# Head sums of a windowed attention by SBUF to SBUF DMA and VectorE adds instead of matmuls, and the softmax in the FFN2 stage

## The chip, the core and the metric

The kernel runs on one core of a Trainium2 chip. Its engines are TensorE (PE in the profile; its weight loads PEld), VectorE (DVE), ScalarE (ACT), GpSimd (POOL) and SyncE (SP, which here only issues DMAs). Each engine works through its own instructions in order, and waits on semaphores for the others. The metric is the device time of one execution in microseconds; the kernel before takes 1237.61 us, the median of three runs (1237.54 to 1237.85).

## What is computed

Two layers, each a windowed self-attention and a feed-forward network, both with a residual and a LayerNorm without scale or shift ahead of them. Sequence S = 2048, width D = 1024, 32 heads of 32, F = 3584, all inputs and the output bf16.

```
def attention(x):                                  # x: layernormed, [S, D]
    q, k, v = split(x @ wqkv)                      # [32 heads, S, 32]
    # token s sees the 8 tokens s, s-2, ..., s-14 (where >= 0)
    logits[h,s,w] = dot(q[h,s], k[h,s-2w]) / sqrt(32)     # else -1e9
    o[h,s] = sum_w softmax_w(logits)[h,s,w] * v[h,s-2w]
    return o.reshape(S, D) @ wo
def ffn(x):
    return gelu_tanh(x @ w1 + b1) @ w2 + b2
for _ in range(2):
    x = x + attention(layernorm(x));  x = x + ffn(layernorm(x))
```

## The kernel before

**Groups and stages.** The 2048 tokens are cut into four groups of T = 512; with two layers there are N = 8 group passes, n = 0 to 7, n mod 4 being the token group. One pass has four stages, each a generator that yields after every unit of TensorE work: gen_qkv (24 units of 8 matmuls: eight chunks of q, of k, of v), gen_wo (8 units of 8 matmuls), gen_ffn1 (28 units of 8), gen_ffn2 (32 units of 7). The stages are interleaved by the loop at the end of the kernel: wo(n), qkv(n+2), ffn1(n), ffn2(n). So the attention of group n+2 is prepared while the FFN of group n runs.

**Attention on VectorE.** The columns of wqkv are taken with a stride of 8, so chunk c of q, k and v holds the channels c, c+8, ... of all heads, and partition p belongs to head p // 4: HP = 4 partitions a head. new_prod(n, c) (L287) multiplies q of a chunk with the eight windows of k, [128 partitions, 8 windows, 512 tokens], into a "big" buffer, and adds the products of the eight chunks up in a tree: 8 multiplications and 7 additions of 4096 elements a partition. What remains is a sum over the four partitions of a head. That is head_sum (L272): eight matmuls with the 0/1 matrix smat, which put token block tb (128 tokens) on the PSUM partitions tb*32 to tb*32+31, one per head, giving L [128, 8, 128]. attend (L349) calls it, and then does the softmax over the windows: maximum, subtraction, exponential (ScalarE), sum, reciprocal and product, into a. spread (L368) copies a through DRAM into abc, so that each of the four partitions of a head has its weights (DMAs issued by POOL). av(n, c) (L381) multiplies abc with the windows of v and adds the eight windows up, into oT.

**Buffers.** "big" has 3 buffers (product tree, av). q, k, abc and oT have one each, v two. The accumulators in PSUM ("acc") are 6, taken in turn by all stages; L has its own. Weights "wt" have 5 buffers of 1 MB.

**Evictions.** gen_ffn2 takes four accumulators for the first half of the columns and four for the second (pss, L443). A half is finished only in its last four units, and VectorE then adds bias and residual: tmp<-acc, x<-tmp.

```
for dh in range(2):
    pss = [[acc_tile() for _ in p] for p in parts]
    for kq in range(4):
        for tt in range(NTT):   # 7 matmuls, one unit
```

**What sets the order.** TensorE's order is the program's: every matmul depends on the one before (L111). On VectorE, ScalarE, POOL and SP a scheduler places instructions, unless the wrapper InOrder (L82) binds them: hold() makes all later instructions of the engine come after the last one so far, and on = True keeps program order (always on for POOL, here). The side work of a stage is hung on units: at(u, f, ...) calls f after unit u, each(f, n, u0, du) calls f(n, c) after unit u0 + du*c. The lines that matter are these (ln_a is the LayerNorm that feeds a qkv, ln_stats_ahead its statistics):

```
stage(gen_ffn1(0), sides=at(4, attend, 1) + at(4, spread, 1) + at(4, hold) + each(new_prod, 2, 2, 1, 0, 4) + each(av, 1, 6, 2))
stage(gen_ffn2(0), sides=at(0, ln_stats_ahead, 3) + at(15, hold) + each(new_prod, 2, 15, 1, 4, 8) + at(23, hold) + at(23, ln_a, 3, None, True))
```

All engine calls go through one-line helpers, so in the profile nearly every instruction has line L93 (InOrder) or L118 (mm); it is told apart by the tiles it writes and reads.

Of the kernel before, what the change touches and what calls it, by code (L numbers as in the profile page):

```python
# [9 lines left out]
ALU = mybir.AluOpType  # L10
AX = mybir.AxisListType
BF16 = mybir.dt.bfloat16
F32 = mybir.dt.float32
# [4 lines left out]
def kernel(  # L18
# [18 lines left out]
    P = 128  # L37
    _, S, D = A_x.shape
    F = B_w1.shape[1]
    H = 32  # L40
    DH = D // H
    W = 8
    DIL = 2
    HALO = (W - 1) * DIL
# [3 lines left out]
    T = 512  # L48
    NTT = T // P
# [4 lines left out]
    HP = P // H  # L54
    N = NLAYER * NG
# [17 lines left out]
    bigp = ctx.enter_context(tc.tile_pool(name="bigp", bufs=3))  # L73
    dram = ctx.enter_context(tc.tile_pool(name="dram", bufs=2, space=bass.MemoryType.DRAM))
    smp = ctx.enter_context(tc.tile_pool(name="smp", bufs=1))
# [51 lines left out]
    def load_qkv(which):  # L127
        tiles = []
        for h in range(2):
            wt = wpool.tile([P, KD // 2, D], BF16, name="wt")  # L130
            sp.dma_start(wt[:], wqkv_v[:, h * (KD // 2):(h + 1) * (KD // 2), which * D:(which + 1) * D])
            tiles.append(wt)
        return tiles
# [121 lines left out]
    def win(t_ap):  # L255
        a = t_ap.ap
        assert len(a) == 2 and a[1][0] == 1 and a[1][1] == HALO + T
        return bass.AP(tensor=t_ap.tensor, offset=t_ap.offset, ap=[list(a[0]), [DIL, W], [1, T]])

    st = {n: {} for n in range(N)}  # L260
    xa = {}
    xb = {}
# [9 lines left out]
    def head_sum(n, last=True):  # L272

        if "L" not in st[n]:
            st[n]["L"] = psum.tile([P, W, P], F32, name="L", bufs=1)
            start = True
        else:
            start = False
        L = st[n]["L"]
        prod = st[n]["prods"].pop(0)  # L280
        for wh in range(2):
            for tb in range(NTT):
                mm(L[tb * H:(tb + 1) * H, wh * 4:(wh + 1) * 4, :], lhsT=smat[:],
                   rhs=prod[:, wh * 4:(wh + 1) * 4, tb * P:(tb + 1) * P], start=start,
                   stop=last, skip_group_check=True, tile_position=(0, tb * H))

    def new_prod(n, c):  # L287

        s = st[n]
        prod = bigp.tile([P, W, T], BF16, name="big")  # L290
        vec.tensor_tensor(out=prod[:], in0=s["qT"][:, c, :].unsqueeze(1).to_broadcast([P, W, T]), in1=win(s["kT"][:, c, :]), op=ALU.mult)
        tree = s["prods"]
        tree.append(prod)
        if c % 2 == 1:
            for _ in range(1 if c % (NCH // s["parts"]) == 1 else 2):
                b = tree.pop()
                vec.tensor_tensor(out=tree[-1][:], in0=tree[-1][:], in1=b[:], op=ALU.add)

    def gen_qkv(n, parts=1, defer=False, qk_pool=None, v_late=False, qk_next=None):
        g = n % NG  # L300
        xnT = xa.pop(n)
        s = st[n]
        s["parts"] = parts
        s["prods"] = []
        qk_pool = qk_pool or attp
        wq = wq_first if n == 0 else load_qkv(0)
        wk = load_qkv(1)
        if n == 0:
            ln_early(1)
            wv = load_qkv(2)  # L310
            ln_early(2, qk_next)
            load_x(3)
        qT = qk_pool.tile([P, NCH, T], BF16, name="qT")
        first = {}
        for kq in range(4 if n == 0 else 0):
            for c in range(6):
                first[c] = qkv_chunk(wq, c, xnT, first.get(c), kq * (KD // 4), (kq + 1) * (KD // 4), 0, 2)
                if (kq, c) in ((1, 5), (2, 5)):
                    transpose_on_pe(*first_late.pop(0))
        for c in range(NCH):  # L320
            ps = qkv_chunk(wq, c, xnT, first[c], t0=2) if c in first else qkv_chunk(wq, c, xnT)
            act.copy(qT[:, c, :], ps[:])
            yield
        if n > 0 and not v_late:
            wv = load_qkv(2)
        kT = qk_pool.tile([P, NCH, HALO + T], BF16, name="kT")
        s["qT"], s["kT"] = qT, kT
        act.copy(kT[:, :, 0:HALO], (zhalo if g == 0 else khalo)[:])
        for c in range(NCH):
            ps = qkv_chunk(wk, c, xnT)  # L330
            act.copy(kT[:, c, HALO:], ps[:])
            if not defer:
                new_prod(n, c)
            yield
        if g + 1 < NG:
            act.copy(khalo[:], kT[:, :, T:T + HALO])
        vT = attp.tile([P, NCH, HALO + T], BF16, name="vT", bufs=2)
        s["vT"] = vT
        if v_late:
            wv = load_qkv(2)  # L340
        act.copy(vT[:, :, 0:HALO], (zhalo if g == 0 else vhalo)[:])
        for c in range(NCH):
            ps = qkv_chunk(wv, c, xnT)
            act.copy(vT[:, c, HALO:], ps[:])
            yield
        if g + 1 < NG:
            act.copy(vhalo[:], vT[:, :, T:T + HALO])

    def attend(n):  # L349

        s = st[n]
        head_sum(n)
        L = s.pop("L")
        if n % NG == 0:
            vec.tensor_tensor(out=L[0:H, 0:W - 1, 0:HALO], in0=L[0:H, 0:W - 1, 0:HALO], in1=mask[:], op=ALU.add)
        mx = smp.tile([P, P], F32, name="mx")
        vec.tensor_reduce(out=mx[:], in_=L[:].rearrange("p w t -> p t w"), axis=AX.X, op=ALU.max)
        e = smp.tile([P, W, P], F32, name="e")
        vec.tensor_tensor(out=e[:], in0=L[:], in1=mx[:].unsqueeze(1).to_broadcast([P, W, P]), op=ALU.subtract)
        act.activation(e[:], e[:], ACT.Exp, scale=SCALE)  # L360
        z = smp.tile([P, P], F32, name="z")
        vec.tensor_reduce(out=z[:], in_=e[:].rearrange("p w t -> p t w"), axis=AX.X, op=ALU.add)
        vec.reciprocal(z[:], z[:])
        a = smp.tile([P, W, P], BF16, name="a")
        vec.tensor_tensor(out=a[:], in0=e[:], in1=z[:].unsqueeze(1).to_broadcast([P, W, P]), op=ALU.mult)
        s["a"] = a
# [45 lines left out]
    def gen_ffn1(n):  # L412
        xnT = xb.pop(n)
        hT = hpool.tile([P, KF, T], BF16, name="hT")
        st[("h", n)] = hT
        for j4 in range(KF // 4):
            wt = wpool.tile([P, KD, 4 * P], BF16, name="wt")
            load = sp.dma_start(wt[:], w1_v[:, :, j4 * 4 * P:(j4 + 1) * 4 * P])
            if n == 0 and j4 == 1:
                dep_order(load, last_transpose[0], "transposes first")  # L420
            for jj in range(4):
                j = j4 * 4 + jj
                ps = acc_tile()
                for k in range(KD):
                    mm(ps[:], lhsT=wt[:, k, jj * P:(jj + 1) * P], rhs=xnT[:, :, k, :], start=(k == 0), stop=(k == KD - 1))
                act.activation(hT[:, j, :], ps[:], ACT.Gelu_apprx_tanh, bias=b1T[:, j:j + 1])
                yield
# [63 lines left out]
    def stage(gen, count=None, sides=()):  # L491


        u = 0
        while count is None or u < count:
            if next(gen, gen) is gen:
                break
            for v, f in sides:
                if v == u:
                    f()  # L500
            u += 1
        for v, f in sides:
            if v >= u:
                f()

    def at(u, f, *args, **kwargs):
        return [(u, lambda: f(*args, **kwargs))]

    def each(f, n, u0, du, c0=0, c1=NCH):
        return [(int(u0 + du * (c - c0)), lambda c=c: f(n, c)) for c in range(c0, c1)]  # L510

    hold = vec.hold
# [5 lines left out]
    with tc.tile_pool(name="early", bufs=1) as early:  # L518
# [10 lines left out]
        hold()  # L529
        stage(q2, sides=each(new_prod, 1, 0, 1, 5, 8))  # L530
    hpool = ctx.enter_context(tc.tile_pool(name="hpool", bufs=1))
    stage(gen_ffn1(0), sides=at(4, attend, 1) + at(4, spread, 1) + at(4, hold) + each(new_prod, 2, 2, 1, 0, 4) + each(av, 1, 6, 2))
    stage(gen_ffn2(0), sides=at(0, ln_stats_ahead, 3) + at(15, hold) + each(new_prod, 2, 15, 1, 4, 8) + at(23, hold) + at(23, ln_a, 3, None, True))
    for n in range(1, N - 2):
        stage(gen_wo(n), sides=at(0, spread, n + 1) if n > 1 else at(7, attend, 2))
        stage(gen_qkv(n + 2), sides=(at(0, spread, 2) if n == 1 else []) + each(av, n + 1, 0, 2, 0, 3))
        stage(gen_ffn1(n), sides=at(20 if n == 1 else 9, attend, n + 2) + each(av, n + 1, 8, 2, 3, 8))
        if n + 3 < N:
            stage(gen_ffn2(n), sides=at(2, ln_a, n + 3))
        else:  # L540
            stage(gen_ffn2(n), sides=at(0, spread, n + 2) + each(av, n + 2, 1, 4))
    n = N - 2
# [35 lines left out]
```

## Time and profile before

| | |
|---|---|
| median of 3 runs | 1237.61 us (1237.54 to 1237.85) |
| profiled execution, its own time | 1237.71 us |
| its span, first to last instruction | 1236.0 us |
| TensorE busy | 1227.6 us, 99% |
| VectorE busy | 840.5 us, 68% |
| ScalarE busy | 303.8 us, 25% |
| GpSimd busy | 92.3 us, 7% |
| head-sum matmuls (64) | 4.9 us |
| HBM read | 197.40 MB |

How to read the lines of the profile: a group is a line, an engine, an operation and what it writes <- what it reads, with partitions x elements and type; then how often, busy time and mean of one, and the idle time of the engine just before, with what ended it. A timeline line begins with start and length in us; consecutive instructions of one kind are merged, and matmul records can be missing by a few per cent. The chain is the work that ended last, followed back from the end. Busy time of TensorE is modelled and doesn't say that it is at its peak.

### The profile page before, as it was taken

Reading aid. Unit: us, or ns where it says so; the run is one execution under the profiler, and the core shown is the slowest. Engines: PE = TensorE matmul, PEld = TensorE weight load, DVE = VectorE, ACT = ScalarE, POOL = GpSimd, SP = SyncE. Lnnn points to the kernel's source line nnn. Section 1 sums busy time; section 2 is a strip of 40 time slices with the busy share of each in tenths; the row PEclk is TensorE's granted clock in tenths of the full one; section 3 lists DMA queues with packets and bytes.
Section 4 is the critical chain, followed back from the end, with each engine's and each line's share of the span. In section 5 each row is a group of like instructions: output and inputs, shape, how many; then the busy total and the mean of one; then the engine's idle time right before and its main releaser. Section 6 shows DMA issues by size and latency. Waiting matters only on the chain.

```text
span 1236.0 us, 13961 instructions
## 1 busy us (share of the span) xinstructions
PE 1227.6 (99%) x5775; PEld 632.1 (51%) x5825; DVE 840.5 (68%) x868; ACT 303.8 (25%) x475; POOL 92.3 (7%) x214
## 2 busy tenths in 40 slices
PE   9999999999999999999999999999999999999998
PEld 6666544456444564445644455444654444444444
DVE  7999899987985899337994379853597787012001
ACT  3333152023420145101351023510234001300310
POOL 4010011002000100001000010000001002000000
PEclk9999999999999999999999999999999999999999
DMA  9954564576645555656556565666554567546441
GB/s 305 283 179 144 187 208 155 166 177 220 183 157 200 168 175 157 195 168 189 166 155 203 171 178 162 162 200 200 171 170 136 185 199 200 162 157 196 150 136 54
DMA packets 217440, 220.33 MB, mean 178 GB/s; under 512 B 68179, under 2 KB 187105, under 8 KB 214305
## 3 DMA queue, kind: packets, MB, share of 16 engines
q1 hardware_dynamic: 214704, 208.69, 54.4%
q0 software_dynamic: 2672, 10.76, 2.9%
q8 instruction: 45, 0.74, 0.2%
q14 instruction: 19, 0.15, 0.0%
HBM read 197.40 MB, written 6.29 MB: 165 GB/s over the span
## 4 chain that ended last, share of the span: by engine, by line
PE 96%; DVE 2%; DMA 1%; issue 0%; POOL 0%; ACT 0%; SPq 0%
PE acc L118 96%; DVE big L93 1%; DVE stats L93 1%; DMA x<-in_A_x_dram 1%; PE L L118 0%; POOL rstd L93 0%; DVE x L93 0%; DVE xn L93 0%; SPq L93 0%; DVE mv L93 0%; ACT xnT L93 0%; PE L L211 0%; ACT kT L93 0%; ACT vT L93 0%; POOL zhalo L93 0%
## 5 line engine op out<-in xcount | busy, mean ns | idle before, releaser
L118 PE MATMUL acc<-xnT,wt 128*128 128x512 bf16 (+1 forms) x3376 | 721.5, 376 | 0.6 <-ACT xnT L93 0.6
L118 PEld LDWEIGHTS <-wt 128*128 128x128 bf16 x3376 | 398.7, 119 | 321.0 <-issue 3.9
L118 PE MATMUL acc<-wt,hT 128*128 128x512 bf16 (+1 forms) x1780 | 386.0, 376 | 2.1
L118 PEld LDWEIGHTS <-hT 128*128 128x128 bf16 x1820 | 178.1, 98 | 209.0
L93 DVE TENSOR_TENSOR big<-big 128x1024 bf16<-128x1024 bf16 (+2 forms) x184 | 244.1, 1358 | 1.8
L93 ACT ACTIVATE hT<-acc,b1T 128x512 bf16<-128x512 f32 x224 | 151.5, 687 | 318.4 <-PE acc L118 317.8
L93 DVE TENSOR_TENSOR big<-abc,vT 128x4096 bf16<-128x4096 bf16 x64 | 143.9, 2282 | 48.2 <-DMA abc<-a_d 47.9
L93 DVE TENSOR_TENSOR tmp<-acc,b2bc 128x512 f32<-128x512 f32 x56 | 38.6, 690 | 179.1 <-PE acc L118 175.7
L93 DVE TENSOR_TENSOR big<-qT,kT 128x4096 bf16<-128x4096 bf16 x64 | 143.8, 2286 | 23.9 <-ACT kT L93 23.2
L93 ACT CAST qT<-acc 128x512 bf16<-128x512 f32 x64 | 37.2, 586 | 324.5 <-PE acc L118 324.5
L118 PE MATMUL acc<-wt,oT 128*128 128x512 bf16 x440 | 97.4, 379 | 0.4
L93 DVE BATCH_NORM_STATS2 stats<-x 128x6 f32<-128x512 bf16 x128 | 83.9, 678 | 4.4 <-DMA x<-in_A_x_dram 3.6
L118 PEld LDWEIGHTS <-oT 128*128 128x128 bf16 x448 | 43.8, 98 | 52.9
L93 DVE TENSOR_TENSOR x<-acc,big 128x512 bf16<-128x512 f32 (+1 forms) x9 | 5.7, 633 | 90.0 <-PE acc L118 90.0
L93 ACT CAST vT<-acc 128x512 bf16<-128x512 f32 x64 | 37.5, 586 | 84.1 <-PE acc L118 84.1
L93 ACT CAST kT<-acc 128x512 bf16<-128x512 f32 x64 | 37.5, 586 | 71.7 <-PE acc L118 71.7
L93 POOL TENSOR_TENSOR rstd<-mv,eps_t 128x1 f32<-128x1 f32 x60 | 14.5, 241 | 500.9 <-DVE mv L93 500.8
L93 POOL DMA_DIRECT2D a_d<-a x32 | 19.0, 620 | 416.3 <-DVE a L93 416.3
L93 DVE TENSOR_TENSOR x<-acc,x 128x512 bf16<-128x512 f32 x64 | 43.0, 671 | 7.8 <-PE acc L118 7.5
L93 DVE TENSOR_SCALAR xn<-x,mv,rstd 128x1024 bf16<-128x1024 bf16 x52 | 28.6, 550 | 27.3 <-POOL rstd L93 26.9
L93 DVE TENSOR_TENSOR x<-tmp,x 128x512 bf16<-128x512 f32 x56 | 38.6, 690 | 1.5
L93 POOL TENSOR_TENSOR rstd<-rstd,mhalf 128x1 f32<-128x1 f32 x60 | 33.8, 563 | 4.7
(54 smaller groups left out, 208.7 us busy)
## 6 DMA issues: line engine op xcount, KB each, us to landing
wt<-in_B_w_dram SPq DMA_DIRECT2D x56, 1024.0 KB, 5.6
wt<-in_B_w_dram SPq DMA_DIRECT2D x64, 896.0 KB, 4.7
wt<-in_A_wqkv_dram SPq DMA_DIRECT2D x46, 1024.0 KB, 5.4
wt<-in_A_wo_dram SPq DMA_DIRECT2D x16, 1024.0 KB, 5.0
abc<-a_d POOLq DMA_DIRECT2D x32, 256.0 KB, 4.4
x<-in_A_x_dram SPq DMA_DIRECT2D x16, 256.0 KB, 6.0
out_dram<-x SPq DMA_DIRECT2D x31, 128.0 KB, 1.7
wt<-in_A_wqkv_dram SPq DMA_DIRECT2D x4, 512.0 KB, 7.8
```

The costliest lines, as they stand in the source:

```text
L93: inst = f(*args, **kwargs)
L118: return pe(nc.tensor.matmul(*args, **kwargs))
```

## The change

Five things are done.

1. Products are stored by token block, [4 blocks, 8 windows, 128 tokens] instead of [8 windows, 512 tokens] (new_prod, win_by_tile, head_sum).
2. For groups 2 to 7 head_sum is no longer called. gather moves the product sum with four DMAs, SBUF to SBUF, so that the four partitions of a head lie beside each other on one partition (Lq [128, 4, 8, 128], a "big" buffer), and attend adds them with three VectorE additions into e (fp32).
3. attend of groups 3 to 6 moves from FFN1 to the start of FFN2; group 7 from unit 9 to unit 20 of FFN1; group 2 stays in wo(1), with a hold ahead of it. attend(1) moves from unit 4 to unit 5 of FFN1(0).
4. All eight products of group 2 are now placed in FFN1(0), ahead of av of group 1 and behind no eviction of FFN2(0); before, the last four were placed behind unit 15 of FFN2(0).
5. The copies of the halos into k and v (groups 3 on) and the exponentials (groups 2 to 6) keep program order on ScalarE.

```diff
+    def win_by_tile(t_ap):
+        a = t_ap.ap
...
+        return bass.AP(tensor=t_ap.tensor, offset=t_ap.offset, ap=[list(a[0]), [P, NTT], [DIL, W], [1, P]])
...
-                   rhs=prod[:, wh * 4:(wh + 1) * 4, tb * P:(tb + 1) * P], start=start,
+                   rhs=prod[:, tb, wh * 4:(wh + 1) * 4, :], start=start,
...
-        prod = bigp.tile([P, W, T], BF16, name="big")
-        vec.tensor_tensor(out=prod[:], in0=s["qT"][:, c, :].unsqueeze(1).to_broadcast([P, W, T]), in1=win(s["kT"][:, c, :]), op=ALU.mult)
+        prod = bigp.tile([P, NTT, W, P], BF16, name="big")
+        q = s["qT"][:, c, :].rearrange("p (b t) -> p b t", t=P)
+        vec.tensor_tensor(out=prod[:], in0=q.unsqueeze(2).to_broadcast([P, NTT, W, P]), in1=win_by_tile(s["kT"][:, c, :]), op=ALU.mult)
...
+        act.on = n > 2
         act.copy(kT[:, :, 0:HALO], (zhalo if g == 0 else khalo)[:])
+        act.on = False
...
+    def gather(n):
+        s = st[n]
+        prod = s["prods"].pop(0)
+        Lq = bigp.tile([P, HP, W, P], BF16, name="big")
+        s["Lq"] = Lq
+        for tb in range(NTT):
+            pool.dma_start(Lq[tb * H:(tb + 1) * H, :, :, :], prod[:, tb, :, :])
...
     def attend(n):
-        head_sum(n)
-        L = s.pop("L")
+        e = smp.tile([P, W, P], F32, name="e")
+        if "Lq" in s:
+            Lq = s.pop("Lq")
+            vec.tensor_tensor(out=e[:], in0=Lq[:, 0, :, :], in1=Lq[:, 1, :, :], op=ALU.add)
+            for j in range(2, HP):
+                vec.tensor_tensor(out=e[:], in0=e[:], in1=Lq[:, j, :, :], op=ALU.add)
+            L = e
+        else:
+            head_sum(n)
+            L = s.pop("L")
...
+        act.on = 1 < n < N - 1
         act.activation(e[:], e[:], ACT.Exp, scale=SCALE)
+        act.on = False
...
-    stage(gen_ffn1(0), sides=at(4, attend, 1) + at(4, spread, 1) + at(4, hold) + each(new_prod, 2, 2, 1, 0, 4) + each(av, 1, 6, 2))
-    stage(gen_ffn2(0), sides=at(0, ln_stats_ahead, 3) + at(15, hold) + each(new_prod, 2, 15, 1, 4, 8) + at(23, hold) + at(23, ln_a, 3, None, True))
+    stage(gen_ffn1(0), sides=at(5, attend, 1) + at(5, spread, 1) + at(5, hold) + each(new_prod, 2, 2, 1)
+          + at(10, gather, 2) + at(10, hold) + each(av, 1, 10, 2))
+    stage(gen_ffn2(0), sides=at(0, ln_stats_ahead, 3) + at(23, hold) + at(23, ln_a, 3, None, True))
     for n in range(1, N - 2):
-        stage(gen_wo(n), sides=at(0, spread, n + 1) if n > 1 else at(7, attend, 2))
+        stage(gen_wo(n), sides=at(0, spread, n + 1) if n > 1 else at(7, hold) + at(7, attend, 2))
         stage(gen_qkv(n + 2), sides=(at(0, spread, 2) if n == 1 else []) + each(av, n + 1, 0, 2, 0, 3))
-        stage(gen_ffn1(n), sides=at(20 if n == 1 else 9, attend, n + 2) + each(av, n + 1, 8, 2, 3, 8))
+        gather(n + 2)
+        stage(gen_ffn1(n), sides=(at(20, attend, n + 2) if n + 3 == N else []) + each(av, n + 1, 8, 2, 3, 8))
         if n + 3 < N:
-            stage(gen_ffn2(n), sides=at(2, ln_a, n + 3))
+            stage(gen_ffn2(n), sides=at(0, attend, n + 2) + at(2, ln_a, n + 3))
```

More of the change, by code (lines that the diff above doesn't have):

```diff
@@ L258, in win @@
         return bass.AP(tensor=t_ap.tensor, offset=t_ap.offset, ap=[list(a[0]), [DIL, W], [1, T]])
+    def win_by_tile(t_ap):
+        a = t_ap.ap
+        assert len(a) == 2 and a[1][0] == 1 and a[1][1] == HALO + T
+        return bass.AP(tensor=t_ap.tensor, offset=t_ap.offset, ap=[list(a[0]), [P, NTT], [DIL, W], [1, P]])
     st = {n: {} for n in range(N)}
@@ L340, in gen_qkv @@
             wv = load_qkv(2)
+        act.on = n > 2
         act.copy(vT[:, :, 0:HALO], (zhalo if g == 0 else vhalo)[:])
+        act.on = False
         for c in range(NCH):
@@ L357, in attend @@
         vec.tensor_reduce(out=mx[:], in_=L[:].rearrange("p w t -> p t w"), axis=AX.X, op=ALU.max)
-        e = smp.tile([P, W, P], F32, name="e")
         vec.tensor_tensor(out=e[:], in0=L[:], in1=mx[:].unsqueeze(1).to_broadcast([P, W, P]), op=ALU.subtract)
+        act.on = 1 < n < N - 1
         act.activation(e[:], e[:], ACT.Exp, scale=SCALE)
+        act.on = False
         z = smp.tile([P, P], F32, name="z")
```

## Prediction

> **What bounds the kernel now.** I read the page first, busy time and the chain of work that ended last.
>
> ```profile
> span 1236.0 us, 13961 instructions
> PE 1227.6 (99%) x5775; PEld 632.1 (51%) x5825; DVE 840.5 (68%) x868; ACT 303.8 (25%) x475; POOL 92.3 (7%) x214
> PE 96%; DVE 2%; DMA 1%; issue 0%; POOL 0%; ACT 0%; SPq 0%
> ```
>
> TensorE is busy all but 8.4 us and carries 96% of the chain. Only two things can move the time: matmuls taken away, and stalls of TensorE added or removed. VectorE's 68% is a mean; whether it becomes late has to be read stage by stage. Next, the groups kept apart by shape (columns: busy us, mean ns | idle before):
>
> ```profile
> L118 PE MATMUL L<-big,smat 128*32 128x512 bf16 x64 | 4.9, 385 | 1.1 <-DVE big L93 1.1
> L93 DVE TENSOR_TENSOR big<-qT,kT 128x4096 bf16<-128x4096 bf16 x64 | 143.8, 2286 | 23.9 <-ACT kT L93 23.2
> L93 DVE TENSOR_TENSOR big<-abc,vT 128x4096 bf16<-128x4096 bf16 x64 | 143.9, 2282 | 48.2 <-DMA abc<-a_d 47.9 <-issue 0.3
> L93 DVE TENSOR_REDUCE mx<-L 128x128 f32<-128x1024 f32 x8 | 9.7, 1217 | 0.0
> L93 DVE TENSOR_REDUCE z<-e 128x128 f32<-128x1024 f32 x8 | 15.4, 1920 | 2.3 <-ACT e L93 2.3
> L93 DVE TENSOR_TENSOR a<-e,z 128x1024 bf16<-128x1024 f32 x8 | 9.7, 1214 | 0.1
> ```
>
> All 64 head-sum matmuls together are 4.9 us: that is the prize. Last, the timeline of TensorE and then of VectorE around FFN1 and FFN2 of group 0, where the change moves products:
>
> ```profile
> 139.19 19.16 PE L118 MATMUL acc<-xnT,wt 128*128 128x512 bf16 x88
> 159.41 0.62 PE L118 MATMUL L<-big,smat 128*32 128x512 bf16 x8 [1.06 <-DVE big L93]
> 199.68 48.51 PE L118 MATMUL acc<-wt,hT 128*128 128x512 bf16 x219
> 248.03 13.98 PE L118 MATMUL acc<-wt,oT 128*128 128x512 bf16 x63
> ```
>
> ```profile
> 169.35 1.92 DVE L93 TENSOR_REDUCE z<-e 128x128 f32<-128x1024 f32 x1 [1.12 <-ACT e L93]
> 187.88 4.50 DVE L93 TENSOR_TENSOR big<-abc,vT 128x4096 bf16<-128x4096 bf16 x2 [0.34 <-issue]
> 221.41 0.76 DVE L93 TENSOR_TENSOR oT<-big 128x512 bf16<-128x512 bf16 x2
> 222.09 0.69 DVE L93 TENSOR_TENSOR tmp<-acc,b2bc 128x512 f32<-128x512 f32 x1
> 227.98 4.49 DVE L93 TENSOR_TENSOR big<-qT,kT 128x4096 bf16<-128x4096 bf16 x2
> 232.50 4.62 DVE L93 TENSOR_TENSOR big<-big 128x4096 bf16<-128x4096 bf16 x2
> 241.56 4.62 DVE L93 TENSOR_TENSOR big<-big 128x4096 bf16<-128x4096 bf16 x2
> 246.09 1.46 DVE L93 TENSOR_SCALAR xn<-x,mv_ahead,rstd_ahead 128x1024 bf16<-128x1024 bf16 x3
> ```
>
> See two things. From 159.4 to 222.1 us VectorE has only 1.12 + 0.34 us of idle time: it is full here. And FFN2's first eviction (tmp<-acc, 222.09) already comes late: the accumulator was ready at about 199.7 + 13 units x 1.51 = 219.3 us.
>
> [...]4096 bf16 elements in 2286 ns, 1024 fp32 in 1214. [...]the first sixteen 128x512 matmuls fill 5.84 us[...]; before shows no long stall afterwards. [...]here a 1024 KB weight load lands 5.6 us after issue.
>
> **Part 1: head sums of groups 2 to 7 leave TensorE.** The chain in order of time gives each block of eight as
>
> ```profile
> 340.40 0.55 PE L L118 x8
> 474.01 0.55 PE L L118 x8
> ```
>
> (start, us), though one matmul reads 385 ns: four run side by side in column strips. 6 x 0.55 = **-3.3 us**; nothing else changes in TensorE's order around them.
>
> **Part 2: the gather and the softmax.** Per group, 1 MB moves SBUF to SBUF in four issues on POOL (0.53 us each by the abc rows, 2.1 us) and lands in an estimated 6 to 10 us. It sits behind the spread of the group before and ahead of the rstd pairs of ln_a; the first of these is needed only some 10 us later, so they wait free. VectorE gains three adds with fp32 output, 1.21 us each by the a<-e,z row, and the max reads SBUF instead of PSUM: 1.92 as z does, not 1.22. That is 3.63 + 0.70 = 4.3 us a group, 26 in all. What hides it: in the period of group 2 VectorE sits idle 12.7, 6.9 and 18.2 us around FFN2. The places I checked for exhaustion of that cover:
> - FFN2(1). Counting from QKV(3)'s start: attention weights a of group 2 end at +19 (before +17; the adds and the slower max come on top), abc lands 12.6 later as before, av 0 to 2 and the products take 46.5 as before (292.2 to 339.1), to +78; five av, three of them one at a time for want of a second buffer, to +101; then adds, max and subtract to +110. First eviction data are ready at 90 + 19.8 = +110 and TensorE needs the slot at 90 + 27.2 = +117. Slack 7 us: 0.
> - FFN1(5), where the exponential of group 7 stands after 19 GELUs: subtract about 953, the GELU of tile 19 at 956, its slot is needed at 957.6. Slack 1.7: 0, up to +2.
> - ScalarE runs in order. The exponential of group 1 now stands behind ten GELUs instead of eight: subtract done about 170.6, table back and GELU of tile 10 done about 175, its slot needed at 177.9. That of group 2 stands among the q copies of QKV(3), done at +12.4 from that stage's start; the slot of the copy behind it is needed at +17.3. Both 0.
> - wo(7) and FFN1(6): av of group 7 starts some 9 us later (abc near 973 against 963.75), a backlog of about 4.5 us when LayerNorm of wo(6) runs; its last transpose lands near 1038 to 1040 against a start at 1038.8. I take **+0.3**, up to +2.
>
> **Part 3: product layout [4,8,128] instead of [8,512].** Inner rows shorten from 512 to 128, still step 1. [...] I take 2286 ns unchanged[...].
>
> **Part 4: head sum of group 1 one unit later.** TensorE reaches it at 158.35 + 1.73 = 160.1, after the sum tile is ready at 159.4. The 1.06 us stall goes: **-1.06**. VectorE does one more product first, and reads L at about 168: no wait.
>
> **Part 5: all eight products of group 2 ahead of av(1).** Before, four products and four adds stood behind FFN2(0)'s first four evictions (227.98 to 246.09 = 18.1 us). In the changed kernel's order every one stands ahead of them, and so do all eight av of group 1 and the statistics, as before. VectorE had no room, so the first eviction starts at 222.1 + 18.1 = 240.2 and ends at 240.9. Who waits: six accumulators rotate. FFN2's first half takes four, the second half two more, and the third tile of the second half (unit 18) needs the first one back; its matmul waits for VectorE in both kernels. TensorE is there at 199.68 - 1.06 + 18 x 1.51 = 225.8 (before 226.9, eviction done at 222.8, so 4.1 us to spare). Stall 240.95 - 225.8 = **+15.1 us**. The fourth tile's slot comes 1.5 us later, just as long as one unit lasts: nothing more. During this, gather(2) holds a big buffer; the av that needs it comes about 14 us after the gather is issued: 0, up to +5.
> After 15 us of idleness [...]the kernel's start showed +2.4[...]. I take **+2.0** (0 to 3.5).
> Afterwards VectorE has caught up (it ends its evictions at 246 and waits for TensorE), so wo(1) starts with no backlog, and weights have had more time.
>
> **Sum.** 1236.0 - 3.3 - 1.06 + 15.1 + 2.0 + 0.3 = 1249.0 span; the profiled execution was 1237.7 for 1236.0, and the median of the runs 1237.6, so +1.6: **1250.6 us**, 1.05% slower.
>
> **Rivals.**
> - *More waits than the one (1257).* Gather blocks a buffer in FFN1(0) (+5), or the 1.7 us margin in FFN1(5) and wo(7) breaks (+2 to 4). For: margins are thin. Against: each has at least some us by the rows. Chance 0.18.
> - [...]Eight products at +2.1 us add 17 us to the stall in FFN2(0), and FFN2(1) with 7 us slack stalls 10 more. [...] Chance 0.05.
> - *Not slower (1234).* The eviction reaches VectorE's front by 225.8. The mechanism: the new layout makes the products and adds of group 2 quicker; it decides where those 15 instructions shrink by 14.4 us, to 1.3 us each from 2.27. Then 1237.6 - 4.4 = 1233.2. [...] Chance 0.03.
> - *The stall is there but smaller (1247)*: [...]VectorE a little quicker. Chance 0.04 below 1247.5.
>
> **How the numbers follow.** The main case, 0.70, has 1250.6 with own range 1248 to 1253. The range has to leave out the 1280s and the not-slower case, and reach into the 1257 case: 1247.5 to 1257. Within 0.2% (2.5 us, about what a measurement of this kernel can tell) ends at 1240.1. Faster 0.03, same 0.01, slower 0.96.
>
> **What would show it.** Head-sum matmuls fall from 64 to 16. One wait of TensorE accumulators on VectorE's tmp or oT work, near 226 us and 15 us long, with matmuls after it slower for some 3 us; first eviction at 240. No 1.06 us wait at 158. Product rows stay at 2286 ns; three e<-big adds a group at 1.21. If TensorE shows no gap there, the step on VectorE being full is wrong; if more gaps appear after 250, the cover of part 2 was wrong.

## The result, and the profile after

The changed kernel takes **1249.72 us** (median of six runs, 1249.35 to 1250.40), the kernel before beside it 1237.83 us (six runs, 1237.54 to 1238.12): a ratio of **1.0097**, with a 95% interval of 1.0084 to 1.0110. It is 12 us slower; 1250.6 was predicted.

The page of the kernel after, busy time and the chain that ended last:

```profile
span 1248.4 us, 13956 instructions
PE 1228.9 (98%) x5777; PEld 632.5 (51%) x5777; DVE 869.8 (70%) x886; ACT 304.6 (24%) x475; POOL 126.3 (10%) x238
PE 93%; DVE 6%; issue 0%; ACT 0%; DVEq 0%
```

TensorE has as much to do as before, but the span is 12.4 us longer, and the chain has 6% of VectorE where it had 2%. VectorE's busy time rose by 29.3 us; that alone says nothing, since it has 379 us of idle time left. The waits of TensorE say where it hurts (us in total, times, longest; two others, of 1.1 and 0.6 us, are at the start and were there before):

```profile
PE acc L118 <- DVE tmp L93: 14.9, 1, 14.9
```

One single wait. The timeline of TensorE in FFN1(0), FFN2(0) and wo(1) (start, length, with the idle time ahead in brackets) gives its place:

```profile
160.10 0.62 PE L118 MATMUL L<-big,smat 128*32 128x512 bf16 x8
160.65 38.16 PE L118 MATMUL acc<-xnT,wt 128*128 128x512 bf16 x176
198.64 27.36 PE L118 MATMUL acc<-wt,hT 128*128 128x512 bf16 x126
240.85 23.54 PE L118 MATMUL acc<-wt,hT 128*128 128x512 bf16 x98 [14.85 <-DVE tmp L93]
264.23 13.98 PE L118 MATMUL acc<-wt,oT 128*128 128x512 bf16 x64
```

126 matmuls are 18 units of 7: the wait is at unit 18 of FFN2(0), where the third tile of the second half takes the accumulator of the first tile again. The head sum of group 1 (160.10) starts without a wait. The same stretch on VectorE:

```profile
196.30 4.62 DVE L93 TENSOR_TENSOR big<-big 128x4096 bf16<-128x4096 bf16 x2
...
239.45 0.75 DVE L93 TENSOR_TENSOR oT<-big 128x512 bf16<-128x512 bf16 x2
240.12 0.68 DVE L93 TENSOR_TENSOR tmp<-acc,b2bc 128x512 f32<-128x512 f32 x1
```

All products of group 2 are done at 200.9, then come the weighted sums of group 1, and the first eviction starts at 240.12 instead of 222.09. The matmul that waits for it starts at 240.85. And in time slices (us, then busy time by engine with the number of instructions, then the granted clock):

```profile
224.00:226.00 2.00, 2.00 (x10) 0.78 (x8) 2.00 (x2) 0.00 (x0) 0.00 (x0) 1.00 0.85 262
228.00:230.00 2.00, 0.00 (x0) 0.00 (x0) 2.00 (x3) 0.00 (x0) 0.00 (x0) 0.58 0.00 0
242.00:244.00 2.00, 2.00 (x6) 0.73 (x5) 1.83 (x4) 0.00 (x0) 0.00 (x0) 0.50 0.00 0
246.00:248.00 2.00, 2.00 (x11) 0.88 (x9) 1.46 (x4) 0.00 (x0) 0.00 (x0) 1.00 0.68 78
```

The clock (third number from the end) is at half from about 228.3 to 245.4; in 242 to 244 six matmuls start where eleven do at full speed. The 98 matmuls behind the wait take 23.38 us (240.85 to 264.23); at 0.2158 each, the pace of the 176 in FFN1(0) (160.65 to 198.64), they would take 21.15. So the slow clock costs 2.23 us more.

Groups of the kernel after, kept apart by shape (busy us, mean ns | idle before):

```profile
L118 PE MATMUL L<-big,smat 128*32 128x512 bf16 x16 | 1.2, 385 | 0.0
L93 DVE TENSOR_TENSOR big<-qT,kT 128x4096 bf16<-128x4096 bf16 x64 | 143.8, 2286 | 26.7 <-ACT kT L93 26.1
L93 DVE TENSOR_TENSOR e<-big 128x1024 f32<-128x1024 bf16 x6 | 7.3, 1218 | 0.0
L93 DVE TENSOR_TENSOR e<-e,big 128x1024 f32<-128x1024 f32 x12 | 14.4, 1202 | 0.1
L93 DVE TENSOR_REDUCE mx<-e 128x128 f32<-128x1024 f32 x6 | 11.5, 1911 | 0.1
```

The products cost what they cost before, to the nanosecond; the additions and the maximum have the expected prices.

### The profile page after: what moved, and what is told of

Read it like the earlier page. It is cut to its first block, busy times and chain, and to the rows that moved or that the text cites. A ratio compares the mean times of both kernels' runs of the same rounds, so it can differ in the third digit from the quotient of the medians.

```text
span 1248.4 us, 13956 instructions
## 1 busy us (share of the span) xinstructions
PE 1228.9 (98%) x5777; PEld 632.5 (51%) x5777; DVE 869.8 (70%) x886; ACT 304.6 (24%) x475; POOL 126.3 (10%) x238
## 4 chain that ended last, share of the span: by engine, by line
PE 93%; DVE 6%; issue 0%; ACT 0%; DVEq 0%
PE acc L118 93%; DVE big L93 5%; DVE stats L93 0%; DVE z L93 0%; DVE oT L93 0%; DVE e L93 0%; DVE a L93 0%; DVE mx L93 0%; PE L L118 0%; ACT e L93 0%; PE acc L211 0%; PE L L211 0%; DVE tmp L93 0%; ACT xnT L93 0%; DVE mv_ahead L93 0%
## 5 line engine op out<-in xcount | busy, mean ns | idle before, releaser
L118 PE MATMUL acc<-wt,hT 128*128 128x512 bf16 (+1 forms) x1820 | 390.5, 377 | 14.9 <-DVE tmp L93 14.9
L93 DVE TENSOR_TENSOR big<-big 128x2048 bf16<-128x2048 bf16 (+2 forms) x184 | 245.5, 1359 | 2.9
L93 DVE TENSOR_TENSOR big<-qT,kT 128x4096 bf16<-128x4096 bf16 x64 | 143.8, 2286 | 26.7 <-ACT kT L93 26.1
L93 POOL TENSOR_TENSOR rstd<-mv,eps_t 128x1 f32<-128x1 f32 x60 | 23.5, 391 | 451.7 <-DVE mv L93 451.6
L93 POOL TENSOR_TENSOR rstd<-rstd,mhalf 128x1 f32<-128x1 f32 x60 | 43.8, 729 | 4.7
L93 POOL DMA_DIRECT2D big<-big x24 | 13.5, 568 | 253.2 <-DVE big L93 236.8
```

The lines of the kernel that those rows point to most:

```text
L93: inst = f(*args, **kwargs)
L118: return pe(nc.tensor.matmul(*args, **kwargs))
```

## Experiments

"Part 5" is the prediction's part 5, point 4 in the list of the change. Point 5 of that list, the program order on ScalarE, stays as it is in the kernel each experiment starts from.

**Part 5 alone** (`only5`), and **part 5 taken back** (`undo5`). `only5` has part 4 in it too (the head sum of group 1 one unit later); `undo5` keeps part 4, and leaves the weighted sums of group 1 hung at unit 10, where the kernel before has unit 6.

```diff
 # only5, in the kernel before
-    stage(gen_ffn1(0), sides=at(4, attend, 1) + at(4, spread, 1) + at(4, hold) + each(new_prod, 2, 2, 1, 0, 4) + each(av, 1, 6, 2))
-    stage(gen_ffn2(0), sides=at(0, ln_stats_ahead, 3) + at(15, hold) + each(new_prod, 2, 15, 1, 4, 8) + at(23, hold) + at(23, ln_a, 3, None, True))
+    stage(gen_ffn1(0), sides=at(5, attend, 1) + at(5, spread, 1) + at(5, hold) + each(new_prod, 2, 2, 1) + at(10, hold) + each(av, 1, 10, 2))
+    stage(gen_ffn2(0), sides=at(0, ln_stats_ahead, 3) + at(23, hold) + at(23, ln_a, 3, None, True))
 # undo5, in the kernel after
-    stage(gen_ffn1(0), sides=at(5, attend, 1) + at(5, spread, 1) + at(5, hold) + each(new_prod, 2, 2, 1)
-          + at(10, gather, 2) + at(10, hold) + each(av, 1, 10, 2))
-    stage(gen_ffn2(0), sides=at(0, ln_stats_ahead, 3) + at(23, hold) + at(23, ln_a, 3, None, True))
+    stage(gen_ffn1(0), sides=at(5, attend, 1) + at(5, spread, 1) + at(5, hold) + each(new_prod, 2, 2, 1, 0, 4) + each(av, 1, 10, 2))
+    stage(gen_ffn2(0), sides=at(0, ln_stats_ahead, 3) + at(15, hold) + each(new_prod, 2, 15, 1, 4, 8) + at(18, gather, 2)
+          + at(23, hold) + at(23, ln_a, 3, None, True))
```

> The kernel before with part 5 alone: all eight products of group 2 ahead of the weighted sums of group 1, head sum 1 one unit later; head sums stay on TensorE for all groups, layout as before. My theory: the stall comes back whole, 1236.0 + 14.9 + 2.2 - 1.1 = 1252.0 span, time about 1253.7, a stall of about 15 us of an FFN accumulator on VectorE's first eviction, near 225 us. Rival, the stall needs the gather or the new layout (part 5 alone is harmless): 1235 to 1240.

Measured: 1253.66 us (1253.00 to 1254.05), span 1251.6; ratio 1.0127 (1.0110 to 1.0144). TensorE's timeline:

```profile
240.48 23.35 PE L118 MATMUL acc<-wt,hT 128*128 128x512 bf16 x98 [14.71 <-DVE tmp L93]
```

The whole loss is there without any gather, new layout or later softmax. Part 5 causes it; part 4, which came along, takes a wait away.

> The kernel after with part 5 alone taken back: the last four products of group 2 stand behind unit 15 of FFN2(0) again, behind its first evictions, and the gather of group 2 follows them. My theory (the loss is one stall of TensorE at unit 18 of FFN2(0), 14.9 us and 2.2 us of a slow clock behind it): both go, the span is 1248.4 - 17.1 = 1231.3 us, the time about 1232.7, 4 to 5 us below the kernel before (six head sums 3.9, the wait ahead of head sum 1 1.1). Rival, something else in the change costs the 12 us (gathers, later softmax, product layout): still 1245 or more. Between them, 1234 to 1240: the attention weights of group 2 come some 4 us later here, and FFN2(1), with about 7 us to spare, runs out of cover.

Measured: **1244.71 us** (1238.22 to 1249.95, 20 runs), span of the profiled one 1236.5; ratio 1.0050 (1.0035 to 1.0065). The median is near the rival's 1245, but neither theory named what is seen: the stall of FFN2(0) is gone, yet instead of 5 us faster than before the kernel is 7 us slower, and its time is spread over 12 us where the kernel before has 0.8. Its profile (of an execution at the low end of this range) has the new waits in wo(1) and at the start of QKV(3), TensorE's timeline:

```profile
246.75 10.52 PE L118 MATMUL acc<-wt,oT 128*128 128x512 bf16 x48
260.10 5.30 PE L118 MATMUL acc<-wt,oT 128*128 128x512 bf16 x16 [2.82 <-DVE tmp L93]
266.14 89.98 PE L118 MATMUL acc<-xnT,wt 128*128 128x512 bf16 x416 [0.75 <-DVE xn L93]
```

and on VectorE, in its timeline, the reason why the evictions were late:

```profile
257.70 0.55 DVE L93 TENSOR_SCALAR xn<-x,mv_ahead,rstd_ahead 128x1024 bf16<-128x1024 bf16 x1 [5.41 <-DMA xnT<-xn]
```

VectorE, in its order, sat for 5.41 us (before: 2.04) in front of the fourth tile of group 3's LayerNorm, which waits until an earlier tile has been transposed by DMA. The gather of group 2, now behind the last product, is issued at 247.9, beside these transpositions. Whether that meeting is the cause, or the added VectorE work, the next two kernels tell.

**Without the gather of group 2** (`heads2`), and **with the transfer alone** (`load2`). Both start from `undo5`.

```diff
 # heads2: group 2 keeps its head sum on TensorE
-    stage(gen_ffn2(0), sides=at(0, ln_stats_ahead, 3) + at(15, hold) + each(new_prod, 2, 15, 1, 4, 8) + at(18, gather, 2)
+    stage(gen_ffn2(0), sides=at(0, ln_stats_ahead, 3) + at(15, hold) + each(new_prod, 2, 15, 1, 4, 8)
 # load2: group 2 keeps its head sum, and its gather is issued but not read
-        prod = s["prods"].pop(0)
+        prod = s["prods"].pop(0) if n > 2 else s["prods"][0]
         Lq = bigp.tile([P, HP, W, P], BF16, name="big")
-        s["Lq"] = Lq
+        if n > 2:
+            s["Lq"] = Lq
```

> As undo5 (part 5 taken back), but group 2 has its head sum on TensorE as before, and no gather; groups 3 to 7 as in the changed kernel. In undo5 the gather of group 2 was issued at 247.9 us, when the LayerNorm of group 3 transposes its tiles into xnT, and VectorE sat 5.4 us behind such a transposition. My theory now: that meeting is what undo5 lost, and what made its time vary. Without it: 1236.0 - 1.1 (wait ahead of head sum 1) - 5 x 0.66 (head sums) + 0.1 = 1231.7 span, 1233.3 in time, varying by no more than the kernel before. Rival, the loss in undo5 is the weighted sums of group 1 hung four units later (first eviction done at 223.9 against 222.8, TensorE there at 225.6): 1236 to 1240 again.

Measured: **1233.35 us** (1233.24 to 1233.78), span 1231.6; ratio 0.9964 (0.9951 to 0.9977). The time is as worked out, and the spread is gone. The weighted sums of group 1 hang four units later here too, so the rival with them is out.

> As heads2, with one transfer added that no one reads: the gather of group 2 is issued behind its last product as in undo5, four DMAs of 256 KB into a free buffer, while the head sum of group 2 stays on TensorE. If the meeting of this gather with the transpositions of group 3 is the cause of undo5's loss: 1 to 13 us above heads2, varying from execution to execution as undo5 did (1238 to 1250). If undo5's loss came from the three adds and the later softmax of group 2 on VectorE: as heads2, within 0.5 us.

Measured: 1245.63 us (1240.10 to 1250.11, 11 runs), 12.3 us above `heads2`; ratio to before 1.0059 (1.0044 to 1.0075). The transfer alone, with nobody to read it, brings back loss and spread. From 246 to 275 us the DMA view (KB each, median us from issue to landing) gives for `load2`

```profile
big<-big POOLq DMA_DIRECT2D x4, 256.0 KB, 14.1
xnT<-xn SPq DMA_TRANSPOSE x7, 6.8
```

and for `heads2`

```profile
xnT<-xn SPq DMA_TRANSPOSE x8, 3.9
```

Both are slower when they meet: the transpositions take 6.8 us instead of 3.9, the gather 14.1 us against 7.6 for the median of all gathers of the kernel after. In the profiled `load2` VectorE waits 6.19 us for xnT<-xn (`heads2` 1.94), TensorE 3.60 us in wo(1) and 1.14 us ahead of QKV(3), and 16 matmuls after the first of these run at 5.30 us instead of 3.45: with 0.44 us from before this stretch that is 7.0 of its 7.1 us of longer span. By what way the two hinder each other no run here shows. Nor is it shown what makes one execution lose 5 to 7 us and another 17. Both profiles are of executions at the low end: `load2` against `heads2` shows that the gather causes the loss, and the profiles show how only for the small losses. Transpositions can be slow without a gather, too: in the changed kernel the four from 246 to 262 us took 6.4 us (median) beside three weight loads of 1 MB; what slowed these was not tested.

So the early place of gather(2) in the changed kernel is worth something: at that place it meets no transposition. The price was paid at another place.

**The lateness kept, the rotation avoided** (`lbanks`, `lbanks2`). The changed kernel with part 5; the last two tiles of FFN2(0)'s second half use the two banks of L, which have been free since the head sum of group 1.

```diff
-            pss = [[acc_tile() for _ in p] for p in parts]
+            if n == 0 and dh == 1:
+                both = psum.tile([P, 2, T], F32, name="L", bufs=1)
+                pss = [[acc_tile()], [acc_tile()], [both[:, 0, :]], [both[:, 1, :]]]
+            else:
+                pss = [[acc_tile() for _ in p] for p in parts]
 # lbanks2, in addition: the eviction of tile 2 is written behind the matmuls of tile 3
+                            late.append((ps, out_cols, xs))
+                            if n == 0 and dh == 1 and tt == 2:
+                                continue
```

> The kernel after, part 5 kept, but the last two token tiles of FFN2(0)'s second half take the two PSUM banks of L, which no one needs after the head sum of group 1, instead of coming back to the accumulators of the first half. VectorE's order is untouched, its first eviction still starts near 240. My theory (the loss comes only through the rotation of six accumulators): no stall at unit 18, and the next need of an accumulator is wo(1), by when VectorE has evicted: span 1248.4 - 17.1 = 1231.3, time 1232.7. Rival, VectorE's lateness is what counts and comes out at the next place (the second half's evictions, wo(1), LayerNorm of group 3): 1238 to 1249, with a wait of TensorE after 240 in place of that at 226.

Measured: 1241.55 us (1240.93 to 1242.22), span 1239.8; ratio 1.0030 (1.0018 to 1.0042). The stall at unit 18 is gone, but TensorE's timeline has another one ahead of the last seven matmuls:

```profile
225.72 3.19 PE L118 MATMUL L<-wt,hT 128*128 128x512 bf16 x14
...
252.02 3.15 PE L118 MATMUL L<-wt,hT 128*128 128x512 bf16 x7 [6.50 <-DVE tmp L93]
```

They write the second bank, and wait for VectorE's reading of the first: both are one tile, and the wait is made for the tile. This was a fault of the experiment.

> As lbanks, but the addition of the bias of the second half's third tile is written behind the matmuls of the fourth. In lbanks the last seven matmuls of FFN2(0) waited 6.5 us for VectorE's reading of the other bank of the same tile, and ran 1.6 us slower after it: an ordering that I had made myself by putting two accumulators into one tile. Theory: with it gone no stall is left, though VectorE's first eviction still starts at 240: span 1239.8 - 8.1 = 1231.7, time 1233.3. Rival, the late VectorE comes out in wo(1) or ahead of QKV(3): 1235 to 1240.

Measured: **1232.84 us** (1232.49 to 1233.00), span 1231.2; ratio 0.9959 (0.9944 to 0.9973). VectorE's order and lateness are those of the changed kernel, in its timeline

```profile
240.22 0.69 DVE L93 TENSOR_TENSOR tmp<-acc,b2bc 128x512 f32<-128x512 f32 x1
```

and yet TensorE waits nowhere in FFN2(0), wo(1) or QKV(3); at unit 18 and at the start of wo(1) its timeline has

```profile
225.96 3.19 PE L118 MATMUL L<-wt,hT 128*128 128x512 bf16 x14
247.11 13.98 PE L118 MATMUL acc<-wt,oT 128*128 128x512 bf16 x63
```

without any idle time ahead. The loss went through the accumulators that come round again, and through nothing else. `lbanks2` is the fastest version measured, 16.9 us below the changed kernel and 4.9 us below the kernel before: six head sums of 0.66, 1.06 for the wait ahead of head sum 1, less 0.14 in FFN1(5), make 4.9.

**How the loss grows with the lateness** (`h2late2`, `h2late4`): `heads2` with redundant multiplications on VectorE ahead of FFN2(0)'s first eviction (the same product written again).

```diff
-        vec.tensor_tensor(out=pv[:], in0=s["abc"][:], in1=win(s["vT"][:, c, :]), op=ALU.mult)
+        for _ in range(3 if (n, c) == (1, 0) else 1):      # h2late4: 5
+            vec.tensor_tensor(out=pv[:], in0=s["abc"][:], in1=win(s["vT"][:, c, :]), op=ALU.mult)
```

> As heads2, with the first multiplication of the weighted sums of group 1 (chunk 0) done three times: 2 x 2.27 us, of which some 4.2 stand ahead of FFN2(0)'s first eviction (one short addition slips behind it). It ends at 223.6 + 4.2 = 227.8, TensorE is there at 225.8: a stall of 2.0 to 2.2. Theory, stall and slow clock are two terms, and the second comes only with a stall of some length (it was there after 2.8 us in undo5 and 4.3 us in h2late4, 1.8 each): heads2 + 2.0 to 2.2, all 98 matmuls behind it at 0.216. Rival, any stall costs the clock too: heads2 + 3.8 to 4.0.

Measured: 1236.70 us (1235.91 to 1237.82), 3.4 above `heads2`: between the two numbers, so the median decides for neither. Profiled, the eviction ends at 228.1 and TensorE stalls 1.92 us at unit 18, close to what was worked out, and 0.59 in wo(1), which was not; the clock is granted in full in every slice from 225 to 234 us. The lateness comes out a second time, in wo(1); of the profiled execution's 3.5 us of longer span, 0.46 lie ahead of FFN2(0), where both kernels are alike, and 0.5 are not in a wait. The clock did not stay full in all executions: the three slowest (1237.40 to 1237.82) have a mean granted clock of 0.998 or 0.999, the other nine 1.000.

> As heads2, with the first multiplication of the weighted sums of group 1 (chunk 0) done five times instead of once: 4 x 2.27 = 9.1 us of work on VectorE ahead of the first eviction of FFN2(0), which ends at about 223.9 in undo5 and is needed at 225.6. Theory: TensorE stalls by what exceeds the 1.7 us, 9.1 - 1.7 = 7.4, near 226, and some 1 to 2.2 us go into a slow clock after it: heads2 + 8.4 to 9.6. Rival, VectorE has other room to take it: less than 4. Rival, the lateness hits again in wo(1): over 11.

Measured: 1240.63 us (1240.06 to 1241.17), 7.3 above `heads2` and below the 8.4 to 9.6 expected. TensorE's timeline:

```profile
230.16 23.11 PE L118 MATMUL acc<-wt,hT 128*128 128x512 bf16 x96 [4.31 <-DVE tmp L93]
257.15 10.52 PE L118 MATMUL acc<-wt,oT 128*128 128x512 bf16 x47 [0.42 <-DVE tmp L93]
```

The stall is 4.31, not 7.4: the scheduler let the eviction pass the tail of the last weighted sum, so that it ends at 230.1, only 6.5 later than in `heads2`. From there the sum holds: 4.31 + 0.42, and 22.95 us for the 98 matmuls of FFN2(0) behind the stall (230.16 to 253.11) instead of 21.15, so 1.80 of slow clock, make 6.5 of 6.9 us of span.

**The cover of part 2** (`double`, `adds2`, `gath2`). In `undo5` (`double`) or `heads2` the new work of each gathered group is done twice.

```diff
 # gath2 (double has both)
+        for _ in range(2):
             for tb in range(NTT):
                 pool.dma_start(Lq[tb * H:(tb + 1) * H, :, :, :], prod[:, tb, :, :])
 # adds2
+            for _ in range(2):
                 vec.tensor_tensor(out=e[:], in0=Lq[:, 0, :, :], in1=Lq[:, 1, :, :], op=ALU.add)
                 for j in range(2, HP):
                     vec.tensor_tensor(out=e[:], in0=e[:], in1=Lq[:, j, :, :], op=ALU.add)
```

> As the kernel with part 5 taken back (undo5), with the gather's four DMAs and the three adds done twice for groups 2 to 7, so that 2.1 us of issues, a second transfer of 1 MB and 3.6 us of VectorE a group are added in the places where the change put its own. My theory, that these are hidden for groups 2 to 6 with some us to spare: nothing there; group 7, whose exponential stands in FFN1(5) with 0.1 us of wait already, stalls by the whole of what is added up to there, 3.6 us and perhaps some of the transfer. So 3 to 6 us over undo5. Rival, the cover is used up in every period: 3 to 6 us in each of six, 18 to 36 in all. Rival, cover is ample everywhere: within 0.5 of undo5.

Measured: 1258.91 us (1256.76 to 1259.75). It told little, since it rests on `undo5`: 4.37 us of its waits are in wo(1) and 7.61 at QKV(3), where the second set of DMAs waited on GpSimd for the first (issued at 259.7 to 266.2, read from GpSimd's timeline; the wait itself has no releaser in the profile) with rstd of the LayerNorm queued behind it (266.8 instead of 260.2). The other 4.2 us are in wo(6). In between there is no wait, but the two parts had to be separated.

> As heads2, with the three additions of groups 3 to 7 done twice: 3.6 us more of VectorE in each of five groups. Theory: hidden for groups 3 to 6 in FFN2. Group 7: the scheduler places its exponential behind 21 GELUs instead of 19, so no wait in FFN1(5); its weighted sums start 3.6 us later, and the last evictions of FFN2(5), which have 2.7 us to spare for the accumulators of wo(6), come late by about 1: heads2 + 0 to 1.5. Rival, the cover is used up in every period: + 18. Rival, it is ample: + 0.

Measured: 1236.22 us (1235.51 to 1239.22), 2.9 above `heads2`. From 60 us to the start of the last group's attention there is no wait of TensorE; the additions of groups 3 to 6 are covered. All three waits that came after that are at the end of the pipeline, 0.28 in FFN1(5), 0.77 in FFN2(5) and 0.74 ahead of FFN1(6): the weighted sums of group 7 started not 3.6 but 8.1 us later (975.0 instead of 966.9). The end of the pipeline was the right place, but the size was missed, and so was the wait in FFN1(5), where none was expected.

> As heads2, with the four gather DMAs of groups 3 to 7 issued twice, the second set into the same buffer behind the first. GpSimd waits for the first set (9.4 us and more in the earlier kernel with doubled gathers) and the data are there some 15 us later. They are issued at the start of FFN1, some 42 us before the softmax of groups 3 to 6 and 30 us before that of group 7, and no LayerNorm transposition runs there. Theory: hidden whole, heads2 + 0 to 0.3 (this against + 12 for one gather of group 2 in load2). Rival, these gathers are near their limit too: + 5 or more.

Measured: 1233.71 us (1233.24 to 1234.12), 0.4 above `heads2`, with executions that overlap. Five doubled gathers away from the transpositions cost next to nothing, one single gather among them 12 us.

## Why the prediction was right

**The stall (part 5), the main term.** Predicted 15.1 us at unit 18, measured 14.85; first eviction predicted at 240.2, measured 240.12. The step "VectorE had no room, so what is moved ahead delays the eviction whole" is confirmed from four sides: part 5 alone gives it (`only5`), without the rotation it costs nothing (`lbanks2`), less lateness gives less (`h2late2`, `h2late4`), and the products have kept their 2286 ns with inner rows of 128, so the rival with products 2.1 us dearer (2.1 was the author's estimate) is out.

**The slow clock.** Taken as 2.0, measured 2.23; that they are so close is in part luck. The 2.0 was the author's estimate from the first 16 matmuls of the kernel before, which fill 5.84 us where 16 of 0.2158 fill 3.45. But the granted clock is 1.00 in every slice from 0 to 8 us there, so the 2.4 us lost are not shown to be a slow clock, and that a stall of TensorE is followed by one was not shown before the change either: the kernel before has no wait of TensorE above 1.1 us. And how much such a stretch costs does not follow from the length of the stall (last section).

**The head sums.** Sized too small: from wo(n) to wo(n+1) it is 152.60 us before and 151.94 after, 0.66 a head sum and not 0.55, 4.0 us in all instead of 3.3. The 0.55 came from the starts in the chain; `lbanks2` and `heads2` confirm the larger number (4.9 and 4.4 us below before).

**The wait ahead of head sum 1.** Gone, 1.06, as predicted.

**The margins of part 2.** 0.3 was taken for wo(7) and FFN1(6) and nothing for FFN1(5); measured 0.14 in FFN1(5) and nothing in wo(7) and FFN1(6). The sum hardly notices, but the place was wrong. FFN2(1), the wo stages and the GELUs showed no wait. The rival "more waits than the one" did not come in the changed kernel. But it was nearer than its text says, and at a place that it did not name: four products later in the order, the gather would have met the transpositions (`undo5`). The gather's landing time, estimated at 6 to 10 us, was 4.0 to 11.3 with a median of 7.6.

**The program order on ScalarE** (point 5 of the list) was given no term. `heads2` and `lbanks2` contain it, and their gains are the head sums and the wait to within 0.1 us, so no cost of it shows.

**The sum.** Measured terms: -4.0 - 1.06 + 14.85 + 2.23 + 0.14 = +12.2, against 12.4 of span and 11.9 between the medians.

The larger mistake was in the first expectation after the prediction: that taking part 5 back would give the whole gain. It took back the stall and moved the gather into the transpositions.

## What to carry to other kernels

Work moved ahead on an engine delays everything behind it by its whole length where that engine has no idle time: here 18.1 us of products and their additions went ahead, and the first eviction came 18.03 us later. The price is that length less the slack of the first consumer, here a stall of 14.85 us, and the consumer to look for is whoever needs the buffer back, not who needs the result. Before moving the work back, look whether another buffer cuts the link: here two idle PSUM banks, with one eviction written a unit later, turned +12 us into -5. And the place of a transfer is chosen by what else is moved at that time: beside a gather that nobody read, the transpositions that the next stage waits for took 6.8 us instead of 3.9 (`load2` against `heads2`).

## What the runs showed of the hardware that was not expected

- In the profiled executions a stall of 1.92 us (`h2late2`) left TensorE's clock at full, one of 2.82 us did not: in `undo5` 16 matmuls after it took 5.30 us instead of 3.45, and the granted clock was 0.50 from 261 to 264 us. The delay was not fixed. By the mean clock of slices of 1 or 2 us it fell 2.3 us after the last matmul in the changed kernel, 3.4 in `undo5`, 4.0 in `lbanks` and 4.6 in `h2late4`; in `undo5` and `h2late4` matmuls were running again by then.
- Once down, the clock stayed at half for 3.4 us in `undo5` and `h2late4`, 6.8 in `lbanks` and 17.1 in the changed kernel, close to one, two and five times 3.4. The cost is what the matmuls under it lose, and it did not grow with the stall: 1.8 us after 2.82 and after 4.31, 2.23 after 14.85, but in `double` 2.9 after 4.37 (16 matmuls in 6.37 us). The stall of 2.82 us thus cost about two thirds of its own length on top.
- One gather of 1 MB beside eight transpositions made the time of the whole kernel vary by 10 to 12 us from one execution to the next (`undo5`, `load2`), where the kernels without this meeting, but for `adds2` (3.7), lie within 2.0. `double`, which has it too, was measured four times only, and lies within 3.0.
- A head sum whose matmuls stand 0.55 us in the chain was worth 0.66 us when it went.
